# Attention and a gated FFN on one core: K and Q transposes in one burst, smaller first loads, a halved last tile

## The chip, the cores and the metric

The kernel runs on one core of a Trainium2 chip. The metric is the device time of one execution in microseconds (us). "Profile" is one execution taken by the hardware profiler; times in it count from the start of the span. The engines are TensorE (PE, with its weight loads as PEld), VectorE (DVE), ScalarE (ACT), GpSimd (POOL) and SyncE (SP). A small q at the end, as in "PEq" or "SPq", means the sequencer of that engine.

## The reference

```
scores = q @ k.T / sqrt(64), causal, plus a bias  -(cum_i - cum_j),  cum = cumsum(max(s, 0))
x      = softmax(scores) @ v          # batch 8, heads 8, 576 tokens, 64 per head
xn     = x / rms(x) * rms_g           # 4608 tokens of 512
out    = (silu(xn @ w_gate) * (xn @ w_val)) @ w_out     # 512 -> 1536 -> 512
```

## The kernel before

A list scheduler on the host (class `Plan`) gets every operation with an engine, a cost in us, a key (lower goes first) and its data dependences. It simulates the engines and the transfers and puts every operation into one fixed order. On the chip each engine then works through its own list strictly in that order. So a cost figure in the source is not work; it is an input to the planning.

The transposes of K and Q of two heads are two bursts of 18 matmuls:

```python
def prep_transpose(b, which, hp, key, eng):        # which: 0 = K, 1 = Q
    p0, dst = KP * which, (KT, QT)[which]           # KP = 64: K in partitions 0-63, Q in 64-127
    t = lay(small_bank(), bf16, "p (c t) -> p c t", n=S, c=KC)
    mms(0.6, [(t[64*j : 64*j+64, c, :], raw[b][p0 : p0+KP, 2*hp+j, c, :], ident_bf[...],
               ...) for c in range(KC) for j in range(2)], key=key)
    # then a copy to KT (VectorE) or QT (ScalarE)
```

The loads at the start, all issued by GpSimd, and the order constraints:

```python
for i in range(2):
    for w in range(2):
        load_runs(0, w, 2*i, 2*i+2, -100 + i)       # K, Q of heads 0-1 and 2-3
for w in range(2):
    load_runs(0, w, 4, 8, -98)                      # K, Q of heads 4-7 in one piece each
ident(ident_bf, -97); ident(ident_F, -96)
load_rows(v_nat[0], v, 0, "pool", -94)              # V in pieces of 128 tokens
# ... gate and value weights in pieces WL = (0, 6, 12) of 128 columns
R.after(vops[2], norms[3])
```

The FFN of a chunk of 512 tokens is FFN1 (gate and value matmuls, tanh on ScalarE, two VectorE steps) and FFN2 (four output tiles of 12 matmuls, one eviction and one store of 256 KB each). Attention of batch b+1 is planned beside the FFN of chunk b. ScalarE also computes the squared norms of K and Q (five activations of about 1.1 us for batch 0, `raw_norm`).

## Time and profile before

| | before |
|---|---|
| time, median of 3 runs | 360.29 us (360.1 to 360.87) |
| span of the profiled run | 358.9 us |
| TensorE busy | 339.0 us |
| first FFN1 matmul | 25.21 us |
| first FFN2 matmul | 57.47 us |
| end of the last matmul | 352.83 us |

Read it in three stretches: up to the first FFN1 matmul (attention of batch 0, with nothing beside it), up to the first FFN2 matmul (weights and batch 1 still arriving), and the rest, where TensorE hardly idles. The lines are in the prediction below.

### The profile page before, as it was taken

The numbers are of one execution on the slowest core, as the hardware profiler recorded it, in microseconds if no ns is written. First come the engines' busy times: TensorE is split into PE (matmuls) and PEld (weight loads), VectorE is DVE, ScalarE is ACT, GpSimd is POOL, SyncE is SP. The second block draws the span as 40 slices with busy tenths as digits, with TensorE's granted clock in tenths as the row PEclk, the third lists the DMA queues.
The fourth block names the chain that finished last, engine by engine and source line by source line (L and its number), as shares of the span: only waits on it lengthen the run. The fifth ranks groups of instructions, "written<-read, shape, count | busy, mean of one in ns | idle before, by whom it ended". The sixth has DMA issues, their size and how long they took to land.

```text
span 358.9 us, 7827 instructions
## 1 busy us (share of the span) xinstructions
PE 339.0 (94%) x2934; PEld 206.7 (58%) x2934; DVE 247.0 (69%) x486; ACT 231.6 (65%) x469; POOL 126.5 (35%) x211
## 2 busy tenths in 40 slices
PE   2969999999999999999999999999999999999993
PEld 2657776698668875888444554445445444444441
DVE  6586965798848992899467967995489538707820
ACT  3858998597678857877677568775876433233311
POOL 8987273301480375117502650357124100000000
PEclk9989999999999999999999999999999999999998
DMA  7999999999999899869978989995801150020011
GB/s 118 211 226 208 216 204 204 172 213 195 203 154 231 170 144 215 189 123 170 207 154 163 182 175 178 164 187 104 177 9 31 55 102 1 1 89 29 0 62 64
DMA packets 138357, 51.14 MB, mean 142 GB/s; under 512 B 127300, under 2 KB 132936, under 8 KB 138312
## 3 DMA queue, kind: packets, MB, share of 16 engines
q1 hardware_dynamic: 131688, 41.13, 60.9%
q0 software_dynamic: 6624, 9.44, 14.4%
q8 instruction: 25, 0.41, 0.5%
q14 instruction: 20, 0.16, 0.2%
HBM read 38.16 MB, written 9.44 MB: 133 GB/s over the span
## 4 chain that ended last, share of the span: by engine, by line
PE 78%; DMA 9%; POOL 6%; DVE 3%; issue 1%; ACT 1%; DVEq 0%; POOLq 0%; ACTq 0%
PE pse L378 12%; PE psa L378 10%; PE psh L378 10%; PE psb L378 10%; PE psf L378 9%; PE psd L378 9%; PE psc L378 9%; PE psg L378 8%; DMA wv_sb<-in_moe_w_val_dram 5%; DMA v_nata<-in_v_dram 4%; POOL v_nata L361 2%; POOL q_nat L361 1%; ACT sq_scr L361 1%; DVE Hs L361 1%; POOL Ee L361 1%
## 5 line engine op out<-in xcount | busy, mean ns | idle before, releaser
L378 PEld LDWEIGHTS <-wv_sb 128*128 128x128 bf16 x624 | 59.9, 98 | 32.9 <-issue 1.3
L378 PEld LDWEIGHTS <-wg_sb 128*128 128x128 bf16 x624 | 59.2, 98 | 30.7 <-issue 0.8
L378 PEld LDWEIGHTS <-Hs 128*128 128x128 bf16 x432 | 41.0, 98 | 45.6
L361 POOL TENSOR_SCALAR_AFFINE_SELECT Ea<-Ea 128x512 bf16<-128x512 bf16 x8 | 5.6, 699 | 61.6 <-ACT Ea L361 61.6
L361 POOL TENSOR_TENSOR vwb<-v_nata,wT 128x512 bf16<-128x512 f32 (+1 forms) x20 | 20.6, 1049 | 6.8 <-DMA v_nata<-in_v_dram 6.8
L378 PE MATMUL pse<-wout_sb,Hs 128*128 128x512 bf16 x96 | 22.5, 379 | 0.0
L378 PE MATMUL psf<-xnT,wv_sb 128*128 128x256 bf16 (+1 forms) x116 | 20.7, 313 | 0.0
L361 ACT ACTIVATE sq_scr<-x_blka 128x512 bf16<-128x512 bf16 x19 | 12.0, 630 | 12.0 <-DVE x_blka L361 11.6
L378 PE MATMUL psc<-xnT,wg_sb 128*128 128x256 bf16 (+1 forms) x104 | 18.8, 316 | 0.0
L361 DVE SCALAR_TENSOR_TENSOR x_blkb<-x_blkb,alb,gB 128x512 bf16<-128x512 bf16 x15 | 11.0, 779 | 10.8 <-POOL alb L361 10.7
L361 ACT ACTIVATE sq_scr<-x_blkb 128x512 bf16<-128x512 bf16 x20 | 12.6, 629 | 7.8 <-DVE x_blkb L361 7.3
L378 PE MATMUL psh<-wout_sb,Hs 128*128 128x512 bf16 x72 | 17.2, 379 | 0.0
L378 PE MATMUL psa<-wout_sb,Hs 128*128 128x512 bf16 x72 | 17.0, 379 | 0.0
L378 PE MATMUL psb<-xnT,wv_sb 128*128 128x256 bf16 (+1 forms) x100 | 16.5, 302 | 0.2 <-DVE u_sbc L361 0.2
L378 PE MATMUL psd<-xnT,wg_sb 128*128 128x256 bf16 (+1 forms) x88 | 16.5, 321 | 0.0
L361 ACT ACTIVATE sq_scr<-q_bf 128x1024 bf16<-128x1024 bf16 (+1 forms) x18 | 16.4, 912 | 0.1
L361 ACT ACTIVATE sq_scr<-k_bf 128x1024 bf16<-128x1024 bf16 (+1 forms) x18 | 16.3, 908 | 0.0
L361 DVE CAST q_bf<-q_nat 128x512 bf16<-128x512 f32 (+1 forms) x30 | 15.3, 510 | 0.9 <-ACT sq_scr L361 0.9
L378 PE MATMUL pse<-xnT,wg_sb 128*128 128x256 bf16 (+1 forms) x92 | 15.5, 305 | 0.0
L378 PE MATMUL psa<-xnT,wg_sb 128*128 128x256 bf16 (+1 forms) x84 | 15.5, 318 | 0.0
L361 POOL TENSOR_TENSOR vwa<-v_nata,wT 128x512 bf16<-128x512 f32 (+1 forms) x15 | 15.1, 1039 | 0.0
L361 DVE CAST k_bf<-k_nat 128x512 bf16<-128x512 f32 (+1 forms) x30 | 13.7, 456 | 0.0
(464 smaller groups left out, 850.4 us busy)
## 6 DMA issues: line engine op xcount, KB each, us to landing
v_nata<-in_v_dram SPq DMA_DIRECT2D x24, 256.0 KB, 5.3
k_nat<-in_k_dram SPq DMA_DIRECT2D x24, 256.0 KB, 3.6
q_nat<-in_q_dram SPq DMA_DIRECT2D x24, 256.0 KB, 4.5
out_dram<-osba SPq DMA_DIRECT2D x12, 256.0 KB, 2.4
out_dram<-osbb SPq DMA_DIRECT2D x12, 256.0 KB, 2.5
out_dram<-osbc SPq DMA_DIRECT2D x12, 256.0 KB, 2.4
v_nata<-in_v_dram POOLq DMA_DIRECT2D x8, 256.0 KB, 10.4
wg_sb<-in_moe_w_gate_dram POOLq DMA_DIRECT2D x2, 768.0 KB, 12.2
```

The costliest lines, as they stand in the source:

```text
L361: o = R.add(eng, us, lambda: f(**{n: real(a) for n, a in kw.items()}), outs, ins, key=key, lat=LAT[eng], kind=kind, dma=dma, name=outs[0]. ...
L378: nc.tensor.matmul(out, lhsT=lhsT, rhs=rhs, start=st, stop=sp)
```

## The change

The intent: a faster start (batch 0 sooner through attention, first weights sooner), fewer TensorE microseconds for the transposes, and a shorter end. The core of the diff:

```diff
-    def prep_transpose(b, which, hp, key, eng):
-        mms(0.6, [... for c in range(KC) for j in range(2)], key=key)
+    def prep_transpose(b, hp, key):
+        t = [lay(bank("kq", 4), ...) for w in range(2)]
+        mms(0.52, [... for c in range(KC) for j in range(2) for w in range(2)], key=key)
...
-            load_runs(0, w, 2 * i, 2 * i + 2, -100 + i)
-        load_runs(0, w, 4, 8, -98)
+    loads = [load_runs(0, w, 2 * i, 2 * i + 2, -100) for i in range(2) for w in range(2)]
+    loads += [load_runs(0, w, 2 * i, 2 * i + 2, -98) for i in (2, 3) for w in range(2)]
+    ident(ident_bf, -98.5)
-    WL = (0, 6, 12)
+    WL = (0, 2, 6, 12)
-    R.after(vops[2], norms[3])
+    for o in vops[2:]:
+        R.after(o, norms[3])
+    # ... masks and alpha of batch 0's first half get key -200; loads in one fixed order
-        mms(0.1 + 0.32 * len(us), ...)   (0.2 / 0.4 AV, 0.24 x transposes, 0.5 scale)
+        mms(0.21 + 0.22 * len(us), ...)  (0.19 / 0.36,  0.22,              0.72)
+        # scale of tokens 128-255 of batch 0 on VectorE; own PSUM group "xt" for x of batch 0
...
     # ffn2, last tile only
+            nh = 2 if c == NCH - 1 and tb == 3 else 1
+            for h in range(nh):    # 12 matmuls, eviction and store of 512 / nh columns
```

## The prediction

> **What bounds the kernel now.** I read the busy rows first, then the list of what TensorE waited for, then the chain that ended last, then the timelines of the first 62 us and the last 10 us. From the page:
>
> ```profile
> PE   2969999999999999999999999999999999999993
> PEclk9989999999999999999999999999999999999998
> DMA  7999999999999899869978989995801150020011
> ```
>
> A slice is 9 us. TensorE is full in every slice but the first, the third and the last, so only the head and the tail can give much. DMA is full in the first six slices too: the head has two limits. The waits of TensorE in the whole run (us in total, times, longest):
>
> ```profile
> PE psa L376 <- POOL ident_bf masks.py:199: 5.8, 1, 5.8
> PE psd L378 <- DVE vwa L361: 2.5, 1, 2.5
> PE psd L376 <- DMA q_nat<-in_k_dram: 0.8, 1, 0.8
> PE psb L378 <- DVE x_blka L361: 0.7, 1, 0.7
> PE psd L378 <- ACT QTa L361: 0.6, 1, 0.6
> ```
>
> Idle is 358.9 - 339.0 = 19.9 us: 5.8 before the first transpose, about 6.1 after the last matmul (352.83 to 358.9), and 8.0 that anyone could still win, 5.8 of it before 60 us. But waits don't show the whole head: until the first FFN matmul TensorE does attention of batch 0, 19.4 us of wall time from 5.79, and what ends that stage is a chain of small steps, not work. In the timeline of TensorE:
>
> ```profile
> 8.29 0.69 PE L376 MATMUL psd<-ident_bf,q_nat 64*64 64x64 bf16 x18 [0.78 <-DMA q_nat<-in_k_dram]
> 25.21 1.26 PE L378 MATMUL psc<-xnT,wg_sb 128*128 128x256 bf16 x8
> 57.47 2.75 PE L378 MATMUL psd<-wout_sb,Hs 128*128 128x512 bf16 x12
> ```
>
> 25.21 is where FFN1 of chunk 0 starts, 57.47 where its FFN2 starts; from there to the tail TensorE runs nearly without a gap. So a head that is n us shorter ends the kernel n us sooner, unless a transfer takes over. The chain shows that this is near (start, us, what):
>
> ```profile
> 18.45 16.26 DMA wv_sb<-in_moe_w_val_dram
> 34.71 0.29 issue
> 35.00 14.99 DMA v_nata<-in_v_dram
> 49.99 0.07 issue
> 50.07 1.04 POOL vwb L361
> ```
>
> **What the Trainium skill says.** (1) "TensorEngine Tiling (Array Packing)", Tile-to-Partition Mapping: in 64x64 mode there are four tiles, one for each pair of SBUF half and PSUM half, and tiles work independently. The old burst keeps K (partitions 0 to 63) or Q (64 to 127) fixed and alternates only the PSUM half: two tiles. The trace agrees, because where a K burst and its Q burst happen to meet the starts get closer:
>
> ```profile
> 40.20 0.38 PE L376 MATMUL psh<-ident_bf,k_nat 64*64 64x64 bf16 x12
> 40.39 0.22 PE L376 MATMUL pse<-ident_bf,k_nat 64*64 64x64 bf16 x2
> 40.41 0.20 PE L376 MATMUL psh<-ident_bf,k_nat 64*64 64x64 bf16 x2
> 40.51 0.35 PE L376 MATMUL pse<-ident_bf,k_nat 64*64 64x64 bf16 x12
> ```
>
> The first 12 starts take 0.19 us (17 ns each). Between 40.39 and 40.51 the trace has 12 starts, K and Q mixed: 10 ns each. (2) "TensorE: Matmul & The Clock Gate", Part 1: an idle array is clocked at half rate and needs a busy window of about 3.4 us to be released. The trace agrees: in the head the 65-wide AV matmuls start 53 ns apart (six in 0.32 us at 15.43), at 21.5 they are 30 ns apart, and after the 2.5 us wait the granted clock is 0.50 from 22.5 to 25.5. (3) "DMA: Bandwidth & Descriptors", Anatomy of one DMA: about 2 us fixed per GpSimd-issued transfer, mostly completion, so small pieces are worse alone. Here the pieces queue behind each other: rates below stay near 330 GB/s of reads, so I expect no loss from cutting 288 KB into 144 KB.
>
> **The change part by part.**
>
> *Loads of batch 0 (on the path).* The landing times of before are:
>
> ```profile
> q_nat<-in_k_dram POOLq DMA_DIRECT2D x1, 288.0 KB, 6.5
> q_nat<-in_q_dram POOLq DMA_DIRECT2D x1, 288.0 KB, 7.5
> wout_sb<-in_moe_w_out_dram POOLq DMA_DIRECT2D x2, 768.0 KB, 17.8
> ```
>
> They were issued at 3.87 and 4.49, so K and Q of heads 4 to 7 landed at 10.4 and 12.0; the Q of heads 2, 3 at about 8.9 (3.30 + 5.6). Cut in four and ordered K, Q, K, Q, the same bytes land at 9.7, 10.5, 11.2 and 12.0: heads 4, 5 are complete 1.5 us sooner, heads 6, 7 not at all. The last pair therefore still starts at 12.0.
>
> *The chain from 12.0 to FFN1, with durations of the trace:* 36 interleaved transposes and drain 0.7; copy of Q on ScalarE 0.65; scores 0.6; two exps 1.1; mask 0.65; AV 0.5; reciprocal and normalisation 0.6; squares 0.8; alpha on GpSimd 1.0; scale 0.72; transposes of x 0.7; two xnT multiplies on VectorE 1.37. Sum 9.4, FFN1 at 21.4. I add 0.6 for collisions on VectorE and for ScalarE (second-half exps of 0.6 can't be interrupted): 22.0. Where do the 3.2 us come from? In before, the Q copies of heads 4 to 7 came at 13.64 and 14.17 behind exps (1 us); the mask of Ec stood behind two V issues of 1.75 us on GpSimd (0.5); the normalisation of AV stood behind V multiplies of 1.28 us (about 1.2, now ordered after the fourth normalisation); both squares were scaled one after the other on ScalarE (0.7, one is now VectorE's). These sum to 3.4.
>
> *First weights.* wv's first 768 KB landed at 25.5 (11.19 + 14.3), just ahead of its use at 26.31. V and the two first weight tiles, 1.18 + 3.15 MB of reads, took 12.0 to 25.5: 320 GB/s. With 256 KB pieces the first gate and value columns need 1.18 + 1.05 MB: landed by 19. The cut is needed, or the faster head would wait for wv. The second pieces (2.1 MB more) land at about 25.2, the third at about 34.8 as now.
>
> *Given back (my estimate).* At 22.0 TensorE has one group of 1.75 us, then two gates, their values at 25.2: to 27.3. Then it needs tokens 256 to 511. Those came 6 to 7 us after the first half in before (xnT at 31.9 and 32.5); I work them out to 28.5. About 1.0 us is lost there.
>
> *Transposes of batch 1 (TensorE is full there).* Six bursts from 38.54 to 45.41 take 0.69, 0.59, 0.40, 0.41, 0.40, 0.41 = 2.9 us. Four bursts of 36 x 10 ns and 0.1 us to switch are 1.85: -1.05. In the head another 1.6 us of TensorE time goes, but only the last pair's 0.45 lay on the path, already in the 9.4.
>
> *The tail.* These rows set the end:
>
> ```profile
> 350.08 2.75 PE L378 MATMUL psb<-wout_sb,Hs 128*128 128x512 bf16 x12
> 352.92 0.60 ACT L361 ACTIVATE osbc<-psb 128x512 f32<-128x512 f32 x1 [2.04 <-PE psb L378]
> 353.54 0.33 SPq L361 DMA_DIRECT2D out_dram<-osbc  x1
> ```
>
> The last tile becomes two of 256 columns. TensorE: 24 matmuls instead of 12; FFN1 shows 8 of 256 at 0.873 against 4 of 512 at 0.864: +0.03. The last eviction: squares of 1024 and 512 elements differ by 0.42 us, so half of 512 saves 0.21. The last store moves 128 KB instead of 256: at 330 GB/s 0.4 less. Sum -0.6.
>
> *The rest.* New cost figures in the host-side scheduler reorder batches 1 to 7; no work is changed. TensorE idles 2.2 us between 60 and 345, so I put 0, plus or minus 1.
>
> Sum: -3.2 + 1.0 - 1.05 - 0.6 = -3.9, and 360.3 - 3.9 = **356.4 us**.
>
> **Rivals.** *(A) Transfers bound the first 55 us.* For it: the chain above is DMA from 18.45 to 50, the bytes before FFN2 of chunk 0 are unchanged, wout's second half lands at 54.4 (36.6 + 17.8). Against: at 50 TensorE still had five sets of eight FFN1 matmuls (4.4 us) that need nothing late, and FFN2 began only at 57.47, 3 us after wout. So about 3 us fit; if the order or the eight outstanding transfers hold something back, the head's gain disappears and the time is about 359. *(B) The half clock takes the place of the wait.* A sparser TensorE before 22 us, or a gap near 27, halves the clock for a window; 3.4 us at half rate costs 1.7, and the result is 358. For it: the 0.50 after 22.5. Against: before pays this too. *(C) All of it adds up:* no starvation near 27 and the reordering closes the later gaps: -3.2 - 1.05 - 0.6 - 2 = 353.4. *(D) The reordering costs:* a new wait of VectorE in the middle; 360 to 361.
>
> **Range and chances.** C is the optimistic end and A the pessimistic, neither likely whole: 353.8 to 358.8. Faster by over 2% means under 353.1, beyond even C: 0.05. Slower by over 2% would take 367 and something broken: 0.01. Within 2%: 0.94.
>
> **What would show it.** Right: last Q transposes of batch 0 start near 12, the first FFN1 matmul near 22 with its value weights landed, FFN2 of chunk 0 near 54 to 55.5, four bursts of 36 at about 0.45 us in batch 1, the last eviction 0.39. Wrong: FFN1 early but FFN2 still at 57 (A); a granted clock of 0.5 for longer than 3 us after 22 (B); TensorE's busy time unchanged at 339 (transposes not faster); gaps after 60 us (D).

## The result

| | before | changed |
|---|---|---|
| time, median | 360.2 us (4 runs) | 357.81 us (4 runs, 356.6 to 358.18) |
| ratio | | 0.9925 (95%: 0.9897 to 0.9953) |
| span of the profiled run | 358.9 | 356.5 |
| TensorE busy | 339.0 | 337.4 |
| first FFN1 matmul | 25.21 | 26.14 |
| first FFN2 matmul | 57.47 | 57.79 |
| end of the last matmul | 352.83 | 352.43 |
| from there to the end of the span | 6.07 | 4.06 |

A ratio here and below is the mean time of one kernel's fast runs over that of the other's fast runs of the same rounds, so not quite the ratio of the medians.

The total is inside the range that was predicted, but the table says that it came another way. The head is not shorter. The 2.4 us between the two profiles are made up so: FFN1 starts 0.9 us later, from FFN1 to FFN2 it takes 0.6 us less, from FFN2 to the last matmul 0.7 us less, and after the last matmul 2.0 us less.

The timeline of TensorE in the changed kernel (start, us, engine, line, operation, count, and in brackets the idle time before it and what ended it), from the first FFN1 group, over the ends of one interleaved burst of batch 1, to the first FFN2 tile:

```profile
26.14 1.83 PE L384 MATMUL psd<-xnT,wg_sb 128*128 128x256 bf16 x8 [0.29 <-DVE xnT L367]
...
43.66 0.21 PE L382 MATMUL psf<-ident_bf,k_nat 64*64 64x64 bf16 x1
...
43.94 0.19 PE L382 MATMUL pse<-ident_bf,k_nat 64*64 64x64 bf16 x1
...
57.79 2.54 PE L384 MATMUL psh<-wout_sb,Hs 128*128 128x512 bf16 x11
```

The burst's 36 starts lie within 0.28 us, 8 ns apart: the interleaving itself works. TensorE's busy time on the K and Q transposes fell from 4.71 to 3.49 us in batch 0 and from 3.29 to 1.81 us in batch 1. The gain of 1.5 us in batch 1 did not bring FFN2 forward, and FFN1 starts late. What TensorE waited for in the changed kernel (us in total, times, longest):

```profile
PE psa L382 <- POOL ident_bf masks.py:199: 5.4, 1, 5.4
PE psd L384 <- DVE vwa L367: 2.3, 1, 2.3
PE psg L384 <- DVE vwa L367: 2.1, 3, 1.4
```

The two lines with vwa are AV matmuls that wait for V times its decay weight, 4.4 us together. Before it was one such wait of 2.5. VectorE's timeline shows why:

```profile
16.67 0.69 DVE L367 TENSOR_TENSOR vwa<-v_nata,pse 128x512 bf16<-128x512 f32 x1 [1.79 <-DMA v_nata<-in_v_dram]
...
21.55 1.87 DVE L367 TENSOR_TENSOR vwa<-v_nata,pse 128x512 bf16<-128x512 f32 x3
23.34 0.75 DVE L367 TENSOR_SCALAR x_blka<-x_blka,ala 128x512 bf16<-128x512 bf16 x1
```

V's second piece of 128 tokens lands at 16.67 (14.38 in before). The other three V multiplies, pushed back by the new order constraint, then run as one block of 1.87 us just ahead of the scale of tokens 128 to 255, which could have run at 22.8 (alpha was done on GpSimd at 22.82).

The change itself made V late: GpSimd now has two more K and Q issues of 0.6 us in front of it, and in this run its work on the identity matrix took 0.8 us longer. V's second piece was issued at 7.13 before and at 9.12 in the changed kernel, and landed 7.2 and 7.5 us after its issue, behind the same bytes.

The clock of TensorE has to be read with care here. The page of the changed kernel shows it as granted in full from the start, but its trace holds no clock record before 27.80, and the page counts such time as full. The pace of the matmuls tells otherwise: the same AV matmuls, before and after that moment in the changed kernel, and eight FFN1 matmuls of before to compare with the group at 26.14 above:

```profile
25.38 0.46 PE L384 MATMUL psb<-vwa,Ef 128*128 128x65 bf16 x5
27.84 0.31 PE L384 MATMUL psh<-vwa,Eg 128*128 128x65 bf16 x5
```

```profile
27.18 1.04 PE L378 MATMUL psd<-xnT,wg_sb 128*128 128x256 bf16 x8
```

So the changed kernel runs at the slow pace up to 27.80, into FFN1. Before had the full clock from 18.85 to 22.27, then 0.50 until 25.68. The first eight FFN1 matmuls took 1.66 us to the next start in the changed kernel, 1.10 in before and 0.87 at full pace.

At the end, the stores of the last 10 us of the span, with the landing time in the last column. First before, then the changed kernel:

```profile
out_dram<-osbb SPq DMA_DIRECT2D x1, 256.0 KB, 2.4
out_dram<-osbc SPq DMA_DIRECT2D x1, 256.0 KB, 3.5
```

```profile
out_dram<-osbb SPq DMA_DIRECT2D x1, 256.0 KB, 2.2
out_dram<-osbc SPq DMA_DIRECT2D x1, 128.0 KB, 2.7
out_dram<-osba SPq DMA_DIRECT2D x1, 128.0 KB, 1.8
```

In before the last store is slow, 3.5 us where the one ahead of it took 2.4. In the changed kernel it is the first half that is slow, 2.7 us for half the bytes, and it is covered; the last half needs 1.8 us. Issued at 353.54 before and at 352.93 after, they land at 357.04 and 354.73.

### The profile page after: what moved, and what is told of

Its sections match the earlier page's. It is cut to its first block, busy times and chain, and to the rows that moved or that the text cites.

```text
span 356.5 us, 7878 instructions
## 1 busy us (share of the span) xinstructions
PE 337.4 (95%) x2946; PEld 205.6 (58%) x2946; DVE 249.8 (70%) x487; ACT 230.5 (65%) x469; POOL 132.9 (37%) x215
## 3 DMA queue, kind: packets, MB, share of 16 engines
q0 software_dynamic: 7712, 9.44, 15.9%
## 4 chain that ended last, share of the span: by engine, by line
PE 79%; DMA 6%; DVE 5%; POOL 4%; issue 3%; ACT 1%; SPq 0%; ACTq 0%; DVEq 0%; POOLq 0%
PE psa L384 11%; PE psd L384 10%; PE psh L384 10%; PE psc L384 10%; PE psb L384 10%; PE pse L384 9%; PE psf L384 9%; PE psg L384 9%; DMA v_nata<-in_v_dram 3%; DMA k_nat<-in_k_dram 2%; POOL q_nat L367 1%; DVE Hs L367 1%; DMA QTb<-q_bf 1%; POOL ala L367 1%; DVE u_sbb L367 1%
## 5 line engine op out<-in xcount | busy, mean ns | idle before, releaser
L367 DVE SCALAR_TENSOR_TENSOR x_blkb<-x_blkb,alb,gB 128x512 bf16<-128x512 bf16 x15 | 12.4, 874 | 11.5 <-POOL alb L367 11.5
L384 PE MATMUL psa<-xnT,wg_sb 128*128 128x256 bf16 (+1 forms) x116 | 19.6, 306 | 0.2 <-DVE u_sbb L367 0.2
L384 PE MATMUL psh<-xnT,wv_sb 128*128 128x256 bf16 (+1 forms) x112 | 19.6, 311 | 0.0
L384 PE MATMUL psd<-wout_sb,Hs 128*128 128x512 bf16 x72 | 17.8, 379 | 0.0
L384 PE MATMUL pse<-xnT,wg_sb 128*128 128x256 bf16 (+1 forms) x96 | 17.5, 317 | 0.0
L384 PE MATMUL psg<-xnT,wv_sb 128*128 128x256 bf16 (+1 forms) x100 | 16.5, 302 | 0.5 <-ACT QTb L367 0.5
L384 PE MATMUL psb<-wout_sb,Hs 128*128 128x512 bf16 (+1 forms) x72 | 15.9, 361 | 0.0
L384 PE MATMUL psc<-xnT,wv_sb 128*128 128x256 bf16 (+1 forms) x92 | 15.5, 305 | 0.3 <-DVE u_sbc L367 0.3
L384 PE MATMUL psc<-xnT,wg_sb 128*128 128x256 bf16 (+1 forms) x84 | 15.5, 318 | 0.0
L384 PE MATMUL psa<-wout_sb,Hs 128*128 128x512 bf16 x60 | 14.6, 379 | 0.0
```

The lines of the kernel that those rows point to most:

```text
L367: o = R.add(eng, us, lambda: f(**{n: real(a) for n, a in kw.items()}), outs, ins, key=key, lat=LAT[eng], kind=kind, dma=dma, name=outs[0]. ...
L384: nc.tensor.matmul(out, lhsT=lhsT, rhs=rhs, start=st, stop=sp)
```

## The experiments

Twelve kernels, all correct. The two theories after the result were: (1) the gain is mostly the tail, and the head got nothing because V came late; (2) the tail is small as predicted, and the transposes or the head did it. Later ones are named where they come up.

### tail_only and no_tail: the last tile alone, and everything else without it

`tail_only` is the kernel before with the new `ffn2`; `no_tail` is the changed kernel with the old `ffn2`. Nothing else is edited. In the traces of `no_tail` and the changed kernel the first 2922 matmuls are the same, one by one, and only the last tile differs (12 matmuls or 24), so in these two the plan is no confounder.

```diff
 tail_only, in before          no_tail, in the changed kernel
+ nh = 2 if last tile else 1   - nh = 2 if last tile else 1
```

> The kernel before with only the last output tile stored in two halves. Theory 1 (most of the gain is at the tail): the two profiles show 6.1 us and 4.1 us from the last matmul's end to the end of the span, so up to -2.0 us, ratio near 0.995 to 0.996. Theory 2 (the prediction's size of the tail: eviction 0.21 and half a store 0.4): -0.6 us, ratio 0.998. The long last landing of before, 3.5 us, may be chance; then theory 2 holds over several runs.

> The changed kernel with the last tile stored whole again. Theory 1: only about 0.5 to 1 us is left of the gain, time near 359.3. Theory 2: about 2 us are left, time near 358.4.

Measured: `tail_only` 359.64 us, ratio to before 0.9958 (0.9938 to 0.9978), about -1.5 us. `no_tail` 359.64 us, ratio 0.9963 (0.9947 to 0.9979), about -1.3 us. The two add up to the 0.9925 of the whole. From the last matmul to the end the profiles show 4.1 us in all halved kernels of that call (`tail_only`, `old_transposes`), and 6.1 us in both that store the tile whole (`no_tail`, `transposes_only`). So the tail is worth 1.5 to 2.0 us, not 0.6, and all the rest of the change about 1.3. Theory 1 holds for the tail and understates the rest.

`no_tail` also gives a free test of the head. It has the plan of the changed kernel, but in its profiled run V landed earlier: AV starts at 16.30 instead of 17.41, FFN1 at 25.03 instead of 26.14, FFN2 at 56.41 instead of 57.79. A head that is 1.1 us shorter brought FFN2 1.4 us forward. It also shows how much landing times vary between runs of one plan. In `no_tail`:

```profile
16.30 0.44 PE L384 MATMUL psd<-vwa,Ea 128*128 128x65 bf16 x5 [1.33 <-DVE vwa L367]
25.03 1.87 PE L384 MATMUL psd<-xnT,wg_sb 128*128 128x256 bf16 x8 [0.29 <-DVE xnT L367]
```

Two later runs, `old_costs` and `norm_early`, have the same order in this stretch. In all four, FFN1 starts 8.73 us after the first AV that needs V's second piece: 17.41 and 26.14, 16.30 and 25.03, 15.91 and 24.64, 15.77 and 24.50. So within this plan V's landing moves FFN1 one for one. (`no_tail`'s profiled run lost time again later, with 3.7 us of TensorE idle from 60 to 340 us where the changed kernel's run of the same plan had 1.2. It is the slowest of its seven, 362.34.)

### two_stores: the whole last tile, stored in two transfers

```diff
-  I("sp", "dma_start", ..., out=out[rows, :], in_=o)
+  for h in range(2):      # last tile only; computed and evicted whole as before
+      I("sp", "dma_start", ..., out=out[rows, cols_h], in_=o[:, cols_h])
```

> The kernel before, its last tile computed and evicted whole, but stored by two transfers of 128 KB. Theory F (the last store of before lands 1.3 us late because the fetch of instructions at the program's end sits on the same transfer engines): the second store still lands 3 us or more after its issue, and the time is that of before, ratio 0.999 to 1.002. Theory S (a smaller last store lands sooner by itself, as the 1.8 us of the changed kernel): landing near 1.8 us, ratio 0.996 to 0.998.

Measured: 359.89 us, ratio 0.9998 (0.9969 to 1.0027). Both halves landed 2.8 us after their issue, between the two forecasts, so neither number was right; the time is that of theory F, though the interval still reaches into theory S's 0.996 to 0.998. A smaller last transfer alone gains nothing that this run can tell from noise.

Why is one store slow? In every profile the slow store is the one whose data move while a 16 KB packet of instructions is fetched. In before the fetch runs from 354.28 to 355.29, after the last store's issue at 353.54; the transfer engines are full from 354.5 to 355.0, and then a small rest goes on until 356.62. In the changed kernel the fetch runs from 352.21 to 353.14: the first half, issued at 351.62, takes 2.7 us, and the last half is free of it. Whole last tiles landed in 3.0 to 3.6 us, halved last pieces in 1.7 to 2.1, in all profiles. The packets in the traces add weight: a store ends with 16 packets of 4 bytes. In before, 14 of the last store's are out by 355.19 and the other two only at 356.25 and 356.61; in the changed kernel, 15 of the first half's are out by 352.96 and the last at 353.85. So one or two of 16 shares lag, not the whole store. No experiment moved the fetch by itself, so that it is the cause stays an inference.

But halving the tile moved it along. In all five profiles with a whole last tile that is stored at once, the fetch starts 0.2 to 0.8 us after the last store's issue. In all eight with a halved tile it starts 0.6 to 0.9 us after the first half's issue, so it falls on the store that is covered. My estimate from these profiles: stores of 256 KB clear of a fetch land in 2.0 us and the last half in 1.8, so 0.2 us of the tail's gain is bytes and 0.2 the smaller eviction. The other 1.5 or so (3.5 against 2.0) would be that the fetch no longer falls on the last store.

### transposes_only and old_transposes: the interleaving alone, and everything but it

```diff
 transposes_only, in before       old_transposes, in the changed kernel
- two prep_transpose per pair     - prep_transpose(b, hp, key)
+ prep_transpose(b, hp, key)      + two prep_transpose per pair
```

> The kernel before with only the interleaved K and Q transposes (both bursts as one, own PSUM group). TensorE's busy time in the four bursts of batch 1 falls from 3.29 to about 1.81 us as in the changed kernel. If TensorE is the bound there, -1.0 to -1.5 us, ratio 0.996 to 0.997; if the transfers of batch 1 set the pace up to 50 us, nothing: ratio 1.000.

> The changed kernel with the separate K and Q bursts of before (so loads, priorities and tail stay changed). Where TensorE is the bound in batch 1: +1.0 to +1.5 us against the changed kernel, near 359. Where transfers set the pace: the same as the changed kernel, near 357.8.

Measured: `transposes_only` 364.24 us, ratio 1.0103 (1.0082 to 1.0124), slower than before by 3.7 us, although TensorE has less to do (busy 337.4 instead of 339.0). `old_transposes` 362.74 us, ratio 1.0048 (1.0023 to 1.0072), slower than the changed kernel by about 4.4 us (1.0048 - 0.9925, times 360). Neither forecast allowed for that. (The edit also moves these transposes to a PSUM group of their own, which no run separates.) The interleaving costs 3.7 us alone and is worth 4.4 us with the rest. TensorE's busy time from 60 to 340 us (stretch, its length, busy, count, clock, DMA share, GB/s) shows where it goes. Before, changed, and `transposes_only`:

```profile
60.00:340.00 280.00, 277.78 (x2148) 1.00 0.73 136
```

```profile
60.00:340.00 280.00, 278.84 (x2151) 1.00 0.70 138
```

```profile
60.00:340.00 280.00, 274.08 (x2154) 1.00 0.76 136
```

Subtract the busy time from 280: TensorE idles 2.2 us in before, 1.2 in the changed kernel and 5.9 in `transposes_only`; `old_transposes` has 4.5. So in these profiles the loss of 3.7 us in `transposes_only` lies in batches 2 to 7, which have no such transposes. (One plan's idle time can differ by 2.5 us between runs, as `no_tail` shows; the median times of the two kernels agree with this reading.) There the same work stands in another order, and more often TensorE comes to an instruction whose input is not ready:

```profile
PE psg L376 <- ACT x_blkb L361: 1.1, 1, 1.1
PE psa L376 <- ACT Eg L361: 1.0, 1, 1.0
PE psh L378 <- DVE Hs L361: 0.7, 1, 0.7
```

### costs_only, trans_costs, old_costs: only the numbers that the planner is given

If the order is a cause of its own (theory P), then edits that change nothing but the cost figures must move the time.

```diff
- mms(0.1 + 0.32 * len(us), items, ...)   # and 0.2 / 0.4, 0.24, 0.5
+ mms(0.21 + 0.22 * len(us), items, ...)  # and 0.19 / 0.36, 0.22, 0.72
```

`costs_only` is this in before, `trans_costs` this in `transposes_only`, `old_costs` the reverse in the changed kernel.

> The kernel before with only the new cost figures of the host-side scheduler (scores, AV, x transposes, scale on ScalarE), so the same work in another order. Theory P (the order planned for batches 1 to 7 is a cause of its own): idle time of TensorE between 60 and 340 us, 2.2 us in before, moves by more than 1 us, and the time with it, up or down. Theory Q (the order hardly matters, as the prediction said with 0, plus or minus 1): ratio 0.997 to 1.003.

> The kernel before with the interleaved transposes and the new cost figures. The transposes alone were 3.7 us slower, with 5.9 us of TensorE idle from 60 to 340. Theory P: the figures bring that idle time down, to about 2 us, and the time to 359 to 361. Theory Q: it stays near 364.

> The changed kernel with the old cost figures. Theory P: idle from 60 to 340 us is above the changed kernel's 1.2 us, by 1 to 4 us, and the time is 359 to 361. Theory Q: 357.8 plus or minus 1.

Measured, ratio to before: `costs_only` 1.0052 (1.0021 to 1.0083), `trans_costs` 1.0045 (1.0012 to 1.0079), `old_costs` 0.9956 (0.9923 to 0.9988). The first says it most plainly: no instruction is added or removed, and the kernel is 1.9 us slower. So theory P holds in kind, the order moves the time by itself. Not in its numbers: `trans_costs` was expected at 359 to 361 and came out at 362.77, and `old_costs`, expected at 359 to 361, has its median at 358.31, with an interval that touches that of the changed kernel. The better figures don't make better plans as a rule. They made a worse one in before, a better one on top of the transposes (1.0045 against 1.0103), and in the changed kernel the difference is not settled. The profiles of this call miss about 30 matmul records each (2905 instead of 2934 in `costs_only`), so I don't compare their idle times closely.

### v_sp: V by another queue

The head: did V come late because GpSimd issued it late, behind eight loads of K and Q (theory V), or because the transfers of the first 17 us are full anyway (theory B)? SyncE's queue is idle at that time.

```diff
-    loads += load_rows(v_nat[0], v, 0, "pool", -94)
+    for sc in range(2):
+        load_row(v_nat[0], v, 0, sc, "sp", -95)
+    loads += [load_row(v_nat[0], v, 0, sc, "pool", -94) for sc in range(2, NB)]
```

> The changed kernel, but the first two 128-row pieces of V of batch 0 come over SyncE's queue, idle at that time, instead of behind eight K and Q issues on GpSimd. Theory V (the late V, landed at 16.7, is what kept the first FFN1 matmul at 25 to 26 us instead of 22): AV starts by 15 instead of 17.4, and the first FFN1 matmul is at 22.5 to 24.5. Theory B (the transfers of the first 17 us are bound by bandwidth, so V first only makes K and Q later): FFN1 still at 25 to 26.5.

Measured: 359.24 us, ratio 0.9972 (0.992 to 1.0024). From TensorE's timeline:

```profile
6.34 0.26 PE L382 MATMUL psa<-ident_bf,q_nat 64*64 64x64 bf16 x1 [6.34 <-DMA q_nat<-in_k_dram]
8.06 0.26 PE L382 MATMUL psb<-ident_bf,q_nat 64*64 64x64 bf16 x1 [1.46 <-DMA q_nat<-in_q_dram]
...
12.12 0.51 PE L384 MATMUL psa<-vwa,Ea 128*128 128x65 bf16 x6 [0.83 <-DVE KTa L367]
...
15.89 0.51 PE L384 MATMUL psb<-vwa,Eb 128*128 128x65 bf16 x6
...
25.68 1.59 PE L384 MATMUL psb<-xnT,wg_sb 128*128 128x256 bf16 x8 [0.18 <-DVE xnT L367]
```

V is there early and the first AV runs at 12.12. The first Q is late for it (its transposes at 8.06 instead of 5.62), the last pair of transposes ends its starts at 15.72 instead of 13.24, and FFN1 starts at 25.68. That is the number of theory B, but not its mechanism. The last load of Q, in the changed kernel (issued at 7.06) and here (issued at 6.34):

```profile
q_nat<-in_q_dram POOLq DMA_DIRECT2D x1, 144.0 KB, 5.7
q_nat<-in_q_dram POOLq DMA_DIRECT2D x1, 144.0 KB, 6.0
```

It lands at 12.8 and at 12.3, and V's second piece lands by 8.5 here. So K, Q and V's first two pieces are together at 12.3 instead of 16.6, and still the last pair is transposed at 15.27: the kernel was planned anew, and in TensorE's list the first AV and more scores, which wait for copies on VectorE, now stand in front of it. The bytes don't hold the last pair here; the order of the engines does. So `v_sp` does not decide between the theories. What speaks for theory V is that V's second piece, behind the same bytes, was issued 2.0 us later in the changed kernel than in before and landed 2.3 us later.

### kq_whole: the last K and Q loads in two pieces again

```diff
- load_runs(0, w, 2 * i, 2 * i + 2, -98) for i in (2, 3) for w in range(2)
+ load_runs(0, w, 4, 8, -98) for w in range(2)
```

> The changed kernel with K and Q of heads 4 to 7 of batch 0 loaded in two pieces as in before (six issues instead of eight, so V is issued 1.2 us sooner). Theory V: V's second piece lands about 1 us sooner and the first AV with it, FFN1 0.5 to 1 us sooner. If the finer pieces help as the prediction said (heads 4, 5 ready 1.5 us sooner, on no path): the total is within 1 us of the changed kernel, apart from what a new order costs later.

Measured: 363.77 us, ratio 1.0093 (1.0032 to 1.0154). V's second piece came no later than 15.9 (its multiplies run from 15.89) and AV started at 17.00 instead of 17.41, FFN1 at 25.75: somewhat earlier, as theory V had it, and it helped little. The loss is again in the plan of the rest: 6.1 us of TensorE idle from 60 to 340, against 1.2. Like the transposes, the piece size can't be judged by the total of a kernel that was planned anew.

### norm_early and v_sp_norm: ScalarE

In the changed kernel ScalarE idles from 23.6 to 28.0, since FFN1 comes late, and is then nearly full until 60. Its waits and its busy time in two stretches:

```profile
ACT T_sba L367 <- PE psd L384: 4.4, 1, 4.4
```

```profile
23.00:29.00 6.00, 1.17 (x2) 1.00 1.18 194
29.00:60.00 31.00, 29.64 (x62) 1.00 1.14 210
```

29.64 of 31 us is 96%. If that holds FFN2 back (theory A), work moved into the hole would bring it forward. The squared norms of batch 0 need only K and Q.

```diff
-    raw_norm(0, 20)
+    raw_norm(0, -61)
```

> The changed kernel with the five squared norms of batch 0's K and Q (5.3 us of ScalarE) given a priority that puts them into ScalarE's holes before 28 us instead of 33 to 42. Theory A (ScalarE, 99% busy from 30 to 60 us and idle for 4.4 us before 28, sets when FFN2 of chunk 0 starts): FFN2 of chunk 0 at 54 to 56 instead of 57.8, time 1 to 3 us under the changed kernel, ratio to before 0.985 to 0.990. Theory D (transfers set it): FFN2 at 57 to 58, time as the changed kernel.

> Both edits. Theories V and A together: FFN1 at 22.5 to 24.5, FFN2 of chunk 0 at 53 to 55, time 354 to 356. If A is wrong: FFN1 early, FFN2 still at 57, and the time of the changed kernel.

Measured: 365.36 us, ratio 1.0133 (1.0082 to 1.0184), and 366.31 us, ratio 1.0158 (1.0107 to 1.0209): both slower than before, against every forecast. The edit did not do what it was meant to. In the list of ScalarE the norms came to stand after the x squares and before the scale of tokens 256 to 575, from 30.92 to 36.27, so the hole stayed (4.46 us before the first tanh) and TensorE got a new one. From the timeline of TensorE, and its stretch of the table by windows (busy us of PE, PEld, DVE, ACT and POOL, then the granted clock):

```profile
37.03 0.40 PE L382 MATMUL psd<-ident_bf,x_blka 128*128 128x128 bf16 x4 [3.02 <-ACT x_blka L367]
```

```profile
36.00:42.00 6.00, 4.21 (x58) 2.95 (x59) 4.27 (x7) 4.86 (x11) 2.41 (x3) 0.69 1.23 211
```

One wait of 3.0 us, then a granted clock of 0.69 here and 0.75 in the next 6 us, and FFN2 starts at 62.56 instead of 57.79. So theory A was not tested. What the run shows is another thing: from FFN1 (24.50 here) to FFN2 it takes 38.1 us, 6.4 more than in the changed kernel. 3.0 of them are the wait. The clock after it accounts for the rest: 6 us at 0.69 and 6 at 0.75 are 3.4 us of full clock lost (an estimate from these two figures). How much theory A could be worth is on record too: from FFN1 to FFN2 TensorE in the changed kernel is busy for 30.45 of 31.65 us, so nothing that it waits for there can cost more than 1.2 us.

## Why the prediction was right, and where it was not

The total was right: 356.4 us with a range of 353.8 to 358.8, and 357.81 measured; "within 2%" with a chance of 0.94. That was in good part luck: the largest term, the head, failed altogether, and a tail of three times the forecast made up for most of it. Its sum, term by term:

- **Head, "-3.2".** This step failed. FFN1 was to start at 22.0 and started at 26.14 (25.03 in another run of the same plan). The flaw is in the sentence "The chain from 12.0 to FFN1". It has the last pair's AV at about 15.7 (12.0 and the five terms before "AV 0.5"), and it ran at 19.63. From there to FFN1 it took 6.5 us, close to the 6.3 of the chain, so the miss of 4.1 us lies almost wholly before that AV. It has two parts. First, V was taken for granted: its second piece, which every AV of the first half needs, landed at 16.6, and the four AVs then ran from 17.41 on, with second-half scores between them in TensorE's list. The prediction had the figures (1.18 MB of V behind K and Q at 320 GB/s), used them for the weights and never put them into the chain. Second, K and Q themselves ran late: the last Q landed at 12.8 and not 12.0, its exps stood behind three others on ScalarE, and the last pair's mask was done at 17.41 and not 15.7. By my estimate V in time would have won 2.2 us at most (the last AV at 17.41 instead of 19.63), so FFN1 at about 23.9 and not 22.0. The V multiplies that were moved out of the way of the normalisation came to stand in the way of the scale (1.87 us at 21.55), so the "1.2" that this constraint was to win was partly paid back three steps later.
- **First weights.** Not contradicted: neither gate nor value weights are among TensorE's waits in the changed kernel. But with FFN1 at 26, the old pieces might have been in time too (wv's first landed at 25.5 in before), so no run shows a gain by it.
- **Given back, "+1.0".** The gap near 27 came as no idle time at all, since FFN1 started late; instead TensorE ran without a gap from 26.14 to 42.70.
- **Transposes of batch 1, "-1.05".** The mechanism was right and the size low: 3.29 to 1.81 us, so -1.5 of TensorE time; 36 starts at 8 ns, not 10. That all of it is worth time in the end is not shown. From FFN1 to FFN2 the profiles have 32.3 us before and 31.7 after (31.4 in `no_tail`), which is 0.6 to 0.9 less. The slower clock at the start of FFN1 takes 0.6 back there (1.66 us for the first eight matmuls, 1.10 in before).
- **Tail, "-0.6".** Right as far as its mechanism goes, but one was missing. The eviction term is exact (0.60 to 0.38, -0.22), and so are the extra matmuls (2.75 to 2.78 from the first start to the last end). The mis-sized term is "at 330 GB/s 0.4 less" for the last store: its landing went from 3.5 to 1.8 us. Clear of a fetch, half the bytes win only 0.2 (2.0 to 1.8); the fetch that no longer falls on the last store is the term that the sum did not have (estimate above). The page's 2.4 is a median over all stores; the last one's own landing, a query away, was not looked up.
- **"The rest, 0, plus or minus 1".** The changed kernel itself is within it: idle from 60 to 340 us fell from 2.2 to 1.2. As a general belief it was wrong. Edits that leave the tail of their base alone moved the time by 1.9 us (`costs_only`) to about 6 (`kq_whole` against the changed kernel), mostly through the plan. The prediction also took its parts to be additive; the interleaving costs 3.7 us in one company and is worth 4.4 in another.
- **Rivals.** A (transfers bind) was not tested in the form written, "FFN1 early but FFN2 still at 57", since FFN1 was not early; in `no_tail` an FFN1 that came 1.1 us earlier brought FFN2 with it. B (half clock) did happen in part, though the clock row of the changed kernel has no slice under 0.9: by the pace of its matmuls the slow clock lasted to 27.80, so longer than the 3 us after 22 that the prediction named as a sign. It cost FFN1's first group 0.8 us against the full pace, where before lost 0.2. `norm_early` shows what B looks like after a gap. D is what the partial versions ran into.

Open: how much of the 1.3 us that `no_tail` keeps is due to the transposes or to the idle time after 60 us. Each is of that size, and single profiles of one plan differ by as much. Open too is whether V would be in time if GpSimd issued it sooner in the same plan, and whether ScalarE costs the stretch from FFN1 to FFN2 any of its 1.2 idle us. No experiment beat the changed kernel.

## What to carry to other kernels

A chain's estimate is only as good as its list of inputs: for each engine step ask which loads it needs besides the one you follow, and put each landing time into the sum. When a host-side planner orders everything, test a part with the plan held as far as possible (like the tail here), because a kernel planned anew differs by several us for reasons that have nothing to do with the part. At the end of a kernel, look up the last store's own landing; halving the last tile so that only a small piece is left after the last matmul gave about 1.5 us here, but by the estimate above only 0.4 us is due to the smaller piece, and the rest to where the instruction fetch fell, which is inferred and may not carry over. And where a clock row shows full speed from the first microsecond, check it against the spacing of equal matmuls.

## What the Trainium skill lacked or had wrong

- "TensorE: Matmul & The Clock Gate", Part 3: it says that matmuls are strictly in program order in start and end. In before, each K burst of 18 comes before its Q burst in program order, and yet at 40.39 the trace has Q matmuls (pse) starting before K matmuls (psh) that start at 40.41, and the two go on alternating up to 40.51. By the profile's records matmuls in different row halves start out of program order.
- The same page, Part 1, gives about 25 ns as the least distance from start to start. That does not hold across tiles; Part 3 of the page itself has about 4 ns from tile to tile, for tiles of 32 rows. For tiles of 64x64, which it does not give: with four in turn the starts are 8 ns apart (36 in 0.28 us at full clock) and about 13 ns at the slow pace of the head (36 from 12.79 to 13.24). A tile by itself still has 32 ns.
- "Runtime: NRT & Kernel Launch", Instruction fetch mechanics, has the refill in blocks of 16 KiB and calls its cost mostly hidden. In all profiles here, the store on which such a fetch falls at the end of the kernel lands late: 3.0 to 3.6 us where a clear one of 256 KB takes 2.0, and 2.7 to 3.1 us for a first half of 128 KB where the second takes 1.7 to 2.1. What a fetch costs a store in flight is on no page.
